# Converting twelve more weight pieces during attention, and moving the second output step, in a fused attention and bilinear FFN kernel on one Trainium2 core

## The chip, the core and the metric

The kernel runs on one core of a Trainium2 chip. The metric is the device time of one execution in microseconds (us). A core has five engines that each take their instructions in a fixed order: PE (TensorE, matrix products), DVE (VectorE), ACT (ScalarE), POOL (GpSimd) and SP (SyncE, which here issues most DMAs). They meet through semaphores: an instruction that waits holds up everything behind it on its engine.

## The reference

```python
scores = scale * q @ k.T                      # 8 batches, 8 heads, 576 tokens, head size 64
mask   = pos[:, None] // 64 >= pos[None] // 64
attn   = softmax(where(mask, scores, -1e9)) @ v
x      = attn.transpose(0, 2, 1, 3).reshape(4608, 512)
out    = ((x @ w_a) * (x @ w_b)) @ w_out      # w_a, w_b: 512 x 1536, w_out: 1536 x 512
```

q, k and v are float32. The three weights arrive as float64, and the kernel turns them into float32 itself, out of the bits. A float32 product is made of three products on PE, of a rounded part (`hi`) and the rest (`lo`) of each operand: hi·hi, hi·lo, lo·hi.

## The kernel before, in words

**Stages.** The 1536 columns of w_a and w_b (and the rows of w_out) are cut into twelve blocks of 128. First comes attention, 64 heads one behind the other; the first pass of the FFN (blocks 0 to 3) is woven into it, so that PE always has products to do between the steps of a head. When attention is over, a rest of the first pass is left (here the tail). Then comes pass 0 (blocks 4 to 7) and pass 1 (blocks 8 to 11), each over six tiles of 768 tokens. A pass reads x and the partial output of the pass before from DRAM and writes its own. In a tile `pair_unit` (L696 to L738) makes 42 products of 384 columns per block, with DVE combining the results in between (the `u_z` operations, L726 to L736), and `pair_out` makes the output product, 96 matmuls (L754), whose results DVE adds to the partial output (L813).

**A head** has four kinds of work. `softmax`: scores on PE (L392, L412), maxima on DVE (L398), exponentials on ACT (L401), the sums' reciprocal `rc` on DVE (L442), then five scalings by `rc` on POOL (L445). `turn`: transposes of the scaled rows on PE (`tp`, L468), a rounded copy `ah` on ACT (L470), the rest `al` on DVE (L472). `values`: the output product in two steps, the first with `ah` (L517), the second with `al` (L521, L523). And the next pairs' K and Q are loaded by SP, split by ACT, DVE and POOL (L337 to L345, K's tile has one buffer) and copied by SP to where PE wants them (L358, L359). The table `SLOT` says in which order a slot of one head calls the steps of its own softmax, of the head before and of the one before that. The framework's scheduler then fixes each engine's order from it.

**Conversion.** A piece is 128 x 512 weights: per block two pieces of w_a and w_b (`KP` = 2) and one of w_out. `fetch` loads it, `convert` takes five DVE instructions (L139, L143, L145, L147, L149) and one of ACT (L140). For w_out, and for blocks 0 to 3, `split` makes hi (ACT) and lo. For w_a and w_b of later blocks `sums` makes four sums of columns (L172) and two instructions for lo (L177, L178). `convert_w` is a generator; each place that calls it lets it go on by a step, which is one DVE instruction or a few. `behind_of` puts a conversion's instruction behind a marked one in DVE's order, without a wait.

**Who converts what, before.** Blocks 0 to 3 in the first slots of attention. w_a and w_b of blocks 4 to 7 (8 pieces) from the end of attention through the tail, then w_out of 4 to 7 (4 pieces) within tile 0 of pass 0. In tiles 1 to 4 of pass 0 the twelve pieces of blocks 8 to 11, which go through a staging tile `st` to DRAM (`wabd`, `wod`) and come back at the end of pass 0. The lines that set the pace:

```python
STEP, STEP2 = 800, 1600                     # ns of PE time per step of conversion
background(min(k * HT / 2.4 / STEP, F2 * PER_F))
conv = convert_w(parts(range(F1 + F2, NF)), nc.vector, paced=True, stage=stage)
SLOT = [(S_, 0, 3), (S_, -1, 0), (T_, -2, 4), (S_, 0, 4), (V_, -2, 3), (S_, 0, 3),
        (T_, -1, 4), (V_, -2, 3), (S_, 0, 3), (T_, -1, 5), (T_, -1, 4)]
```

Of the kernel before, what the change touches and what calls it, by code (L numbers as in the profile page):

```python
# [41 lines left out]
STEP2 = 1600  # L42
# [10 lines left out]
def attention_then_bilinear_ffn(  # L53
# [33 lines left out]
    wod = dram.tile([F2, P, 2 * DO], F32, name="wod")  # L87
# [39 lines left out]
    def convert(raw, nm, paced):  # L127

        hi, mid = raw[:, :, 1], raw.bitcast(U16)[:, :, 1]
        s, m, x = (wpool.tile([P, 512], I32, tag=f"cv_{x}", name=f"{x}{nm}") for x in "smx")  # L130
        sf, mf, xf = (t.bitcast(F32) for t in (s, m, x))
        v = nc.vector

        def step(ins):
            if paced:
                behind_of(ins, "hf")
# [12 lines left out]
        step(v.tensor_tensor(xf, mf, sf, op=ALU.mult))  # L149
        return xf, mf  # L150
# [4 lines left out]
    def parts(fs):  # L155
        return [(f, i) for f in fs for i in range(KP)] + [(f, KP) for f in fs]
# [4 lines left out]
    def sums(hi, lo, xf, t, paced):  # L161
# [11 lines left out]
        if paced:  # L173
            behind_of(ins, "hf")
        nc.scalar.copy(hi[:, 3:], t)
        yield
        v.tensor_tensor(lo[:, :3], x[:, 1:], f32(hi[:, :3]), op=ALU.subtract)  # L177
        v.tensor_tensor(lo[:, 3:], t, f32(hi[:, 3:]), op=ALU.subtract)  # L178

    def convert_w(todo, lo_eng, paced=False, stage=None):  # L180
# [5 lines left out]
        for k, (f, i) in enumerate(todo):  # L186
            now, raw = raw, ahead(*todo[k + 1]) if k + 1 < len(todo) else None
            xf, spare = yield from convert(now, f"w{f}_{i}", paced)
            if stage:
                st = stage.tile([P, 2, NW if i < KP else NO, P], F32R, tag="st", name=f"st{f}_{i}")  # L190
            if i == KP:
                if not stage and w_sb[f][1] is None:
                    new_wo(f)
                o = st.rearrange("p j c n -> p j (c n)") if stage else w_sb[f][1]
# [383 lines left out]
    n_moe = n_conv = 0  # L578
# [4 lines left out]
    def want(now):  # L583

        n = (now - H - LAG) * per_slot - behind
        if now < 2 * H + LAG:
# [9 lines left out]
            (T_, -1, 4), (V_, -2, 3), (S_, 0, 3), (T_, -1, 5), (T_, -1, 4)]  # L596
    fill = sum(m for _, _, m in SLOT)
    gens = {}
    for s in range(NH + LAG):
# [11 lines left out]
        for g, m in steps:  # L611
# [43 lines left out]
    upool = pool(right, "upool", 2, "right", reuse_waits="tile")  # L655

# [113 lines left out]
    conv = convert_w(parts(range(F1, F1 + F2)), nc.vector, paced=True)  # L770
# [16 lines left out]
    stage = pool(left, "stage", 1, reuse_waits="tile")  # L787
# [12 lines left out]
    for ps_ in range(2):  # L800
        fs = list(range(F1 + ps_ * F2, F1 + (ps_ + 1) * F2))
        for tt in range(NT2):
# [19 lines left out]
            for i, f in enumerate(fs):  # L822
# [13 lines left out]
                if ps_ == 0 and tt == NT2 - 1:  # L836
                    new_w(f + F2)
# [7 lines left out]
            if ps_ == 0 and tt == 0:  # L845
                background(1e4)
                conv = convert_w(parts(range(F1 + F2, NF)), nc.vector, paced=True, stage=stage)
                n_conv, start, k, pace = 0, 0, 0, STEP2
            pair_out(fs, hs, nm, out)
            if ps_ == 0 and tt == NT2 - 1:  # L850
                background(1e4)
                for f in fs:
                    new_wo(f + F2)
                    nc.sync.dma_start(f32(w_sb[f + F2][1]).rearrange("p j n -> p (j n)"), wod[f - F1])
# [39 lines left out]
```

## Time and profile before

| | us |
|---|---|
| median of three runs | 1281.07 (1278.56 to 1282.27) |
| the profiled execution, its own time | 1281.83 |
| its span, first to last instruction | 1279.8 |
| PE busy | 1239.3 (97%) |
| DVE busy | 999.2 (78%) |
| ACT busy | 683.6 (53%) |
| POOL busy | 554.9 (43%) |

The times are of one profiled execution. A busy engine has an instruction in work; PE's instructions overlap, so a busy PE may still be slower than it could be, and the number of matmuls in a stretch tells more. Idle time of an engine that nobody waits for costs nothing. Attention takes about half of the span, the tail some 70 us, pass 0 the stretch from 699 us to 1000 us, and pass 1 the rest.

### The profile page before, as it was taken

How to read it: one execution, taken by the hardware profiler on the slowest of the kernel's cores; microseconds unless marked ns; L12 is line 12 of the kernel's file. 1: busy time of each engine (PE TensorE's matmuls, PEld its weight loads, DVE VectorE, ACT ScalarE, POOL GpSimd, SP SyncE). 2: the span in 40 equal slices, each digit the busy share in tenths (PEclk: the TensorE clock that was granted, in tenths of full speed). 3: DMA queues.
4: the chain of work that ended last, by engine and by line, in shares of the span. 5: the costliest groups of instructions: out<-in, count | busy, mean ns of one | idle time of the engine just before them, and what ended most of it. 6: DMA issues, size and time to landing. Idle time of an engine off the chain costs nothing.

```text
span 1279.8 us, 23524 instructions
## 1 busy us (share of the span) xinstructions
PE 1239.3 (97%) x7849; PEld 1173.2 (92%) x7849; DVE 999.2 (78%) x2389; ACT 683.6 (53%) x1722; POOL 554.9 (43%) x679
## 2 busy tenths in 40 slices
PE   9988999999999999999988998999999999999998
PEld 5668998999999999999988998999999999999998
DVE  6878887777887877877699999899967577577553
ACT  5788787788787788888745423233222222122210
POOL 4567565566665565665422322223223123123231
PEclk8999999999999999999998999999999999999999
DMA  5467766777767767676225355364466442243131
GB/s 195 132 167 201 187 174 175 178 171 181 170 167 179 179 171 176 167 178 155 87 94 171 100 180 194 139 206 164 141 220 244 145 149 79 70 149 98 52 99 62
DMA packets 93496, 196.58 MB, mean 154 GB/s; under 512 B 11968, under 2 KB 52928, under 8 KB 93376
## 3 DMA queue, kind: packets, MB, share of 16 engines
q1 hardware_dynamic: 88768, 185.64, 51.4%
q10 hardware_dynamic: 4608, 9.44, 2.0%
q8 instruction: 63, 1.03, 0.3%
q14 instruction: 57, 0.47, 0.1%
HBM read 96.47 MB, written 47.19 MB: 112 GB/s over the span
## 4 chain that ended last, share of the span: by engine, by line
PE 71%; DVE 15%; DMA 4%; issue 4%; ACT 3%; POOL 2%; SPq 1%; ACTq 0%; DVEq 0%; POOLq 0%
PE pso_z L754 13%; PE ps L217 12%; PE tp L468 7%; PE psx_z L708 6%; PE psw_z L708 6%; PE psv_z L708 6%; PE pso L217 4%; PE s L392 4%; PE psy_z L708 3%; PE av L517 3%; PE av L523 3%; PE sl L392 2%; DMA kp<-kT 2%; PE av L507 2%; DVE sw L147 1%
## 5 line engine op out<-in xcount | busy, mean ns | idle before, releaser
L113 POOL TENSOR_TENSOR h_z<-u_z,h_z 128x384 fp32r<-128x384 f32 x96 | 112.8, 1175 | 391.4 <-ACT h_z L110 379.8
L217 PE MATMUL ps<-xh,wab 128*128 128x288 f32 x1024 | 241.8, 304 | 1.2 <-ACT a L241 1.2
L754 PE MATMUL pso_z<-h_z,wo 128*128 128x384 f32 x1152 | 204.0, 335 | 4.5 <-POOL h_z L113 4.5
L445 POOL TENSOR_SCALAR e<-e,rc 128x512 f32<-128x512 f32 (+3 forms) x256 | 151.6, 604 | 127.9 <-DVE rc L442 118.1
L754 PEld LDWEIGHTS pso_z<-h_z,wo 128*128 128x128 f32 x1152 | 199.6, 188 | 7.0 <-POOL h_z L113 7.0
L217 PEld LDWEIGHTS ps<-xh,wab 128*128 128x128 f32 x1024 | 172.3, 189 | 4.7 <-ACT a L241 1.4
L472 DVE TENSOR_TENSOR al<-tp,ah 128x512 fp32r<-128x512 f32 x224 | 131.6, 608 | 31.5 <-ACT ah L470 31.0
L217 PE MATMUL ps<-xl,wab 128*128 128x288 f32 x512 | 154.1, 301 | 0.0
L468 PE MATMUL tp<-ident,e 128*128 128x128 f32 x832 | 136.1, 278 | 10.4 <-POOL e L445 4.0
L470 ACT CAST ah<-tp 128x512 fp32r<-128x512 f32 x224 | 116.4, 531 | 50.3 <-PE tp L468 47.5
L110 ACT CAST h_z<-u_z 128x384 fp32r<-128x384 f32 x96 | 49.3, 514 | 167.7 <-DVE u_z L733 160.2
L217 PE MATMUL pso<-hh,wo 128*128 128x288 f32 x512 | 128.1, 311 | 4.3 <-ACT hh L110 4.3
L708 PE MATMUL psx_z<-xh,wab 128*128 128x384 f32 x384 | 118.5, 344 | 7.2 <-DVE u_z L726 6.7
L468 PEld LDWEIGHTS tp<-ident,e 128*128 128x128 f32 x832 | 100.8, 142 | 25.7 <-POOL e L445 9.5
L401 ACT ACTIVATE e<-s,nm 128x192 f32<-128x192 f32 (+2 forms) x192 | 101.5, 529 | 32.4 <-DVE nm L398 23.2
L708 PE MATMUL psw_z<-xh,wab 128*128 128x384 f32 x384 | 117.0, 340 | 0.8 <-DVE u_z L728 0.8
L708 PE MATMUL psv_z<-xh,wab 128*128 128x384 f32 x384 | 116.7, 339 | 0.5 <-DVE u_z L730 0.4
L398 DVE TENSOR_REDUCE nm<-s 128x1 f32<-128x192 f32 (+3 forms) x256 | 109.9, 431 | 2.4
L217 PEld LDWEIGHTS ps<-xl,wab 128*128 128x128 f32 x512 | 96.5, 188 | 3.4
L217 PEld LDWEIGHTS pso<-hh,wo 128*128 128x128 f32 x512 | 88.3, 192 | 6.6 <-ACT hh L110 5.3
L113 POOL TENSOR_TENSOR v<-vr,v 128x320 fp32r<-128x320 f32 x56 | 50.2, 897 | 89.3 <-ACT v L110 67.9
L392 PE MATMUL s<-k,q 128*128 128x256 f32 x336 | 81.2, 322 | 2.2 <-ACT e_s L401 1.9
(142 smaller groups left out, 2919.5 us busy)
## 6 DMA issues: line engine op xcount, KB each, us to landing
k<-kp SPq DMA_DIRECT2D x112, 288.0 KB, 3.8
xr<-xd SPq DMA_DIRECT2D x48, 384.0 KB, 3.5
pt<-part SPq DMA_DIRECT2D x96, 192.0 KB, 3.5
q<-qp SPq DMA_DIRECT2D x112, 160.0 KB, 2.6
raww<-wab SPq DMA_DIRECT2D x24, 512.0 KB, 3.8
qp<-qT SPq DMA_DIRECT2D x32, 320.0 KB, 3.2
vr<-vm SPq DMA_DIRECT2D x64, 160.0 KB, 3.1
kp<-kT SPq DMA_DIRECT2D x32, 288.0 KB, 3.5
```

Source lines behind the costliest of these rows:

```text
L110: nc.scalar.copy(hi, src)
L113: return lo_eng.tensor_tensor(lo, src, f32(hi), op=ALU.subtract)
L217: mm = nc.tensor.matmul(ps, w_, d_, start=(i == 0), stop=(i == n - 1))
L392: mark = nc.tensor.matmul(ps[:, :w], qm[:, q0[t]:q0[t] + P], kk[:, :w], start=(i == 0), stop=(i == len(ks) - 1))
L398: nc.vector.tensor_reduce(nm[:, t:t + 1], view, axis=AX.X, op=ALU.max, negate=True)
L401: nc.scalar.activation(out, view, AF.Exp, bias=bias, accum_out=sm[:, t, :1])
L445: nc.gpsimd.tensor_scalar(ev, ev, rc[:, t:t + 1], 1.0, op0=ALU.mult, op1=ALU.mult)
L468: mark = nc.tensor.transpose(tp[:, c], src, ident)
L470: nc.scalar.copy(ah[:, :m, cols], tp[:, :m])
L472: return nc.vector.tensor_tensor(al[:, :m, cols], tp[:, :m], f32(ah[:, :m, cols]), op=ALU.subtract)
L708: nc.tensor.matmul(ps, wt[:, i, iw], j[:, ix], start=start and kp == 0 and i == 0 and j is xh, stop=kp == KP - 1 and i == 1, skip_group_ch ...
L754: nc.tensor.matmul(ps, wt[:, a, osl], b, start=i == 0, stop=i == 3 * len(fs) - 1)
```

## The change

Twelve of the twenty-four later pieces are converted during attention and kept in DRAM: w_out of blocks 4 to 11 (8 pieces) and w_a, w_b of blocks 8 and 9 (4 pieces). A new generator `convert_to_dram` does it, from slot 13 to the last, by steps spread evenly, behind the marked `rc`. It has no tile of its own: hi is written to the second buffer of the raw tile, lo in place over the converted values, and both are stored by SP in two or three DMAs. w_out of blocks 4 to 7 is then loaded by `load_wo`. In pass 0 only w_a, w_b of blocks 10 and 11 (4 pieces) are left, at 3000 instead of 1600 ns per step. In `SLOT` the second step of `values` of the head before last now stands in front of a step of `turn` of the last head, instead of behind it.

```diff
-STEP2 = 1600
+STEP2 = 3000
...
-    wod = dram.tile([F2, P, 2 * DO], F32, name="wod")
+    wod = dram.tile([2 * F2, P, 2 * DO], F32, name="wod")
...
+    def convert_to_dram(todo, paced):
+
+        for f, i in todo:
+            raw = fetch(wab[f, :, i] if i < KP else wo[f], f"w{f}_{i}")
+            yield
+            xf, spare = yield from convert(raw, f"w{f}_{i}", paced)
+            n = f"st{f}_{i}"
+            hi = wpool.tile([P, 2 * NO, P], F32R, tag="raw", name=n, bufs=2)
+            if i == KP:
+                hi = hi[:, :NO].rearrange("p c n -> p (c n)")
+                lo = xf.bitcast(F32R)
+                split(hi, lo, xf, nc.scalar, nc.vector)
+                nc.sync.dma_start(wod[f - F1, :, :DO], f32(hi))
+                nc.sync.dma_start(wod[f - F1, :, DO:], f32(lo))
+            else:
+                hi = hi[:, :NW]
+                lo = yield from sums(hi, None, xf, spare, paced)
+                to = wabd[f - F1 - F2, i]
+                nc.sync.dma_start(to[:, :NW * P], f32(hi).rearrange("p c n -> p (c n)"))
+                nc.sync.dma_start(to[:, NW * P:][:, :3 * P], f32(lo[0]).rearrange("p c n -> p (c n)"))
+                nc.sync.dma_start(to[:, (NW + 3) * P:], f32(lo[1]).rearrange("p c n -> p (c n)"))
+            yield
...
+    HALF = F1 + F2 + F2 // 2
+    later = convert_to_dram(parts(range(F1, NF), [KP]) + parts(range(F1 + F2, HALF), range(KP)), "rc")
+    LATER_FROM, LATER_STEPS = 13, 2 * F2 * 6 + F2 // 2 * KP * 7
...
-            (T_, -1, 4), (V_, -2, 3), (S_, 0, 3), (T_, -1, 5), (T_, -1, 4)]
+            (V_, -2, 3), (T_, -1, 4), (S_, 0, 3), (T_, -1, 5), (T_, -1, 4)]
...
+            while k in (6, 9) and n_later < LATER_STEPS * (now - LATER_FROM) / (NH - 1 - LATER_FROM):
+                next(later, None)
+                n_later += 1
...
+    def load_wo(f):
+        new_wo(f)
+        nc.sync.dma_start(f32(w_sb[f][1]).rearrange("p j n -> p (j n)"), wod[f - F1])
...
-    conv = convert_w(parts(range(F1, F1 + F2)), nc.vector, paced=True)
+    conv = convert_w(parts(range(F1, F1 + F2), range(KP)), nc.vector, paced="hf")
...
+    for f in range(F1, F1 + F2):
+        load_wo(f)
...
-                conv = convert_w(parts(range(F1 + F2, NF)), nc.vector, paced=True, stage=stage)
+                conv = convert_to_dram(parts(range(HALF, NF), range(KP)), "hf")
```

What this does to the engines' orders is shown at three places. Names carry buffer numbers, which differ between the two programs, and the change's lines are about 20 to 35 higher.

PE in the slot of a head in the middle of attention, before: `s` are scores, `ps` products of the first pass, `tp` transposes of the last head, `av` the output product of the head before it.

```order
L392 MATMUL s_0_4618<-k_0_4405,q_0_4404 128x320 x2
L217 MATMUL ps_2_1_1_4678<-xh_0_1_2656,wab_81 128x288
L217 MATMUL ps_2_1_1_4678<-xh_1_1_2974,wab_81 128x288
L217 MATMUL ps_2_1_1_4678<-xl_1_1_2975,wab_81 128x288
L468 MATMUL tp_7_3_4695<-ident,e_3_120 128x128 x4
L217 MATMUL ps_2_1_1_4678<-xh_1_1_2974,wab_81 128x288
L217 MATMUL ps_2_1_1_4678<-xh_2_1_3292,wab_81 128x288
L217 MATMUL ps_2_1_1_4678<-xl_2_1_3293,wab_81 128x288
L217 MATMUL ps_2_1_1_4678<-xh_2_1_3292,wab_81 128x288
L521 MATMUL av_6_4706<-ah_6_4534,v_6_4491 128x128
L521 MATMUL av_6_4706<-al_6_4535,v_6_4491 128x128
L523 MATMUL av_6_4670<-al_6_4535,v_6_4491 128x256
```

The same engine in the same slot with the change:

```order
L542 MATMUL av_6_4767<-ah_6_4634,v_6_4564 128x128
L542 MATMUL av_6_4767<-al_6_4635,v_6_4564 128x128
L544 MATMUL av_6_4744<-al_6_4635,v_6_4564 128x256
L544 MATMUL av_6_4744<-al_6_4635,v_6_4564 128x320
L544 MATMUL av_6_4744<-al_6_4635,v_6_4564 128x448
L544 MATMUL av_6_4744<-al_6_4635,v_6_4564 128x512
L238 MATMUL ps_2_1_1_4752<-xh_1_1_2994,wab_81 128x288
L238 MATMUL ps_2_1_1_4752<-xh_2_1_3321,wab_81 128x288
L238 MATMUL ps_2_1_1_4752<-xl_2_1_3322,wab_81 128x288
L489 MATMUL tp_7_3_4792<-ident,e_3_120 128x128 x4
```

The six matmuls of the second output step, which stood behind the first four transposes, now stand in front of them.

DVE in that slot with the change, from the last `al` of one head to the first maximum behind it (`xf` and `avlo` belong to `values`, `hf` to the first pass, `xw` and the line with `st` to a w_out piece):

```order
L493 TENSOR_TENSOR al_6_4635<-tp_6_0_4721,ah_6_4634 128x2x128
L451 MEMSET s_0_4692 64x64
L359 SCALAR_TENSOR_TENSOR qp_2_4360<-qp_2_4360 128x640
L419 TENSOR_REDUCE nm_0_4688<-s_0_4692 128x1
L549 TENSOR_TENSOR xf_3_4743<-av_6_4767,avlo_6_4774 64x64
L550 TENSOR_TENSOR avlo_6_4774<-av_6_4767,avlo_6_4774 64x64
L149 TENSOR_TENSOR xw_2_4307<-mw_2_4306,sw_2_4305 128x512
L552 TENSOR_TENSOR avlo_6_4774<-avlo_6_4774 64x64
L553 TENSOR_TENSOR xf_3_4743<-av_6_4744,avlo_6_4774 64x512
L493 TENSOR_TENSOR al_7_4791<-tp_7_3_4792,ah_7_4790 128x4x128
L113 TENSOR_TENSOR xw_2_4307<-xw_2_4307,st_2_4782 128x512
L451 MEMSET s_0_4808 64x64
```

Two conversion instructions (L149 and L113) are added in this slot; both stand behind the `al` that the second output step needs, and the rest of the work is as before. On ACT, the copy of K (L344) stands behind the first transpose copy of a head in twenty pairs before, and behind the third or the last with the change.

DVE in tile 0 of pass 0, second block, before (`u_z` combines products of `pair_unit`; `sw`, `mw`, `xw` and the line that writes `wo` are the conversion of w_out):

```order
L726 TENSOR_TENSOR u_z_0_5_10719<-psx_z_0_5_10676,u_z_0_5_10719 128x384
L113 TENSOR_TENSOR wo_10652<-xw_2_10614,wo_10652 128x512
L736 TENSOR_TENSOR u_z_0_4_10628<-psx_z_0_4_10561,u_z_0_4_10628 128x384
L139 TENSOR_SCALAR sw_2_10680<-raww_2_10610 128x512
L143 TENSOR_SCALAR mw_2_10681<-raww_2_10610 128x512
L728 TENSOR_TENSOR u_z_0_5_10720<-psw_z_0_5_10677,u_z_0_5_10719 128x384
L145 SCALAR_TENSOR_TENSOR mw_2_10681<-raww_2_10610,mw_2_10681 128x512
L147 SCALAR_TENSOR_TENSOR sw_2_10680<-raww_2_10610,sw_2_10680 128x512
L730 TENSOR_TENSOR u_z_0_5_10720<-psv_z_0_5_10678,u_z_0_5_10720 128x384
```

And with the change (`xt` and `xr` prepare the next tile's x):

```order
L760 TENSOR_TENSOR u_z_0_5_10888<-psx_z_0_5_10857,u_z_0_5_10888 128x384
L762 TENSOR_TENSOR u_z_0_5_10889<-psw_z_0_5_10858,u_z_0_5_10888 128x384
L764 TENSOR_TENSOR u_z_0_5_10889<-psv_z_0_5_10859,u_z_0_5_10889 128x384
L709 TENSOR_TENSOR xt_1_1_11079<-xr_1_10854,xr_1_10852 128x384
L710 TENSOR_TENSOR xr_1_10852<-xr_1_10852 128x384
```

The conversion has left the stretch between the combining steps. Over pass 0, DVE's order holds 30, 23, 29, 26, 16 and 0 conversion rows in tiles 0 to 5 before, and 2, 12, 16, 10, 0 and 0 with the change. The tail's order differs by four rows, the switch from pass 0 to pass 1 by none.

## Rows read from the trace of the kernel before

**Rows 1.** Busy time by stretch: attention; pass 0, tiles 0 to 4; a tile of pass 1.

```profile
core 0: us, PE busy (x) PEld busy (x) DVE busy (x) ACT busy (x) POOL busy (x), PEclk, DMA share, GB/s
218.00:618.00 400.00, 398.20 (x2871) 381.98 (x2870) 316.86 (x1006) 320.50 (x903) 245.03 (x350) 1.00 0.68 169
...
699.00:747.00 48.00, 47.11 (x264) 45.70 (x263) 47.62 (x83) 19.46 (x33) 14.65 (x11) 1.00 0.44 142
747.00:800.00 53.00, 47.64 (x266) 45.51 (x266) 48.97 (x86) 17.63 (x30) 13.58 (x10) 1.00 0.53 176
800.00:848.50 48.50, 47.26 (x265) 45.49 (x264) 43.66 (x76) 15.55 (x27) 13.52 (x10) 1.00 0.49 157
848.50:897.40 48.90, 47.32 (x267) 45.62 (x266) 46.53 (x81) 17.05 (x29) 13.49 (x10) 1.00 0.54 187
897.40:945.80 48.40, 47.48 (x266) 45.60 (x265) 41.62 (x63) 13.11 (x23) 13.47 (x10) 1.00 0.47 151
...
1043.90:1090.40 46.50, 46.50 (x267) 46.33 (x266) 31.37 (x51) 11.37 (x20) 13.14 (x10) 1.00 0.35 107
```

**Rows 2.** Groups by line and shape, whole span: busy us, mean ns of one.

```profile
L145 DVE SCALAR_TENSOR_TENSOR mw<-raww,mw 128x512 f32<-128x512 uint16 x36 | 32.5, 902 | 0.4
L147 DVE SCALAR_TENSOR_TENSOR sw<-raww,sw 128x512 int32<-128x512 int32 x36 | 29.9, 829 | 0.7 <-ACT sw L140 0.6
L149 DVE TENSOR_TENSOR xw<-mw,sw 128x512 f32<-128x512 f32 x36 | 28.2, 783 | 0.7
L140 ACT ACTIVATE sw<-sw,shift 128x512 int32<-128x512 int32 x36 | 26.0, 723 | 13.7 <-DVE sw L139 13.3
L143 DVE TENSOR_SCALAR mw<-raww 128x512 int32<-128x512 int32 x36 | 23.2, 644 | 0.1
L139 DVE TENSOR_SCALAR sw<-raww 128x512 int32<-128x512 int32 x36 | 20.0, 556 | 0.1
L172 DVE TENSOR_TENSOR mw<-xw 128x128 f32<-128x128 f32 x32 | 9.0, 320 | 0.2
L178 DVE TENSOR_TENSOR st<-mw,st 128x512 fp32r<-128x512 f32 x8 | 5.8, 726 | 0.2 <-ACT st L175 0.2
L177 DVE TENSOR_TENSOR st<-xw,st 128x384 fp32r<-128x384 f32 x8 | 4.4, 546 | 0.0
L113 DVE TENSOR_TENSOR st<-xw,st 128x512 fp32r<-128x512 f32 x4 | 2.8, 690 | 0.3 <-ACT st L110 0.3
```

**Rows 3.** Waits of DVE in attention, 218 to 618 us: us, times, longest.

```profile
DVE al L472 <- ACT ah L470: 20.7, 25, 1.2
DVE s L413 <- PE s L412: 15.6, 30, 1.1
DVE avlo L531 <- ACT avlo L530: 7.7, 18, 0.7
DVE xf L528 <- ACT avlo L527: 7.1, 19, 0.4
DVE nm L398 <- PE sl L392: 4.7, 30, 0.2
```

**Rows 4.** Timeline of one head's slot: start us, us, instruction, idle before.

```profile
524.08 0.19 DVE L442 RECIPROCAL rc<-rc 128x5 f32<-128x5 f32 x1
524.19 0.98 DVE L472 TENSOR_TENSOR al<-tp,ah 128x512 fp32r<-128x512 f32 x2
...
524.37 1.31 POOL L445 TENSOR_SCALAR e<-e,rc 128x512 f32<-128x512 f32 x2 [3.14 <-DVE rc L442]
...
525.71 0.60 PE L468 MATMUL tp<-ident,e 128*128 128x128 f32 x4
526.68 0.22 PE L521 MATMUL av<-ah,v 128*128 128x128 f32 x1
```

**Rows 5.** One POOL group at 60 to 112 us and at 218 to 618 us.

```profile
L445 POOL TENSOR_SCALAR e<-e,rc 128x448 f32<-128x448 f32 x5 | 4.5, 907 | 0.0
...
L445 POOL TENSOR_SCALAR e<-e,rc 128x448 f32<-128x448 f32 x41 | 26.3, 641 | 0.0
```

**Rows 6.** DMA issues, whole span: count, KB each, median us to landing.

```profile
raww<-wab SPq DMA_DIRECT2D x24, 512.0 KB, 3.8
```

More of the change, by code (lines that the diff above doesn't have):

```diff
@@ L135, in step @@
             if paced:
-                behind_of(ins, "hf")
+                behind_of(ins, paced)
         step(v.tensor_scalar(s, hi, 20, 0x7FF, op0=ALU.logical_shift_right, op1=ALU.bitwise_and))
@@ L153, in attention_then_bilinear_ffn, with parts @@
     w_sb = {}
-    def parts(fs):
-        return [(f, i) for f in fs for i in range(KP)] + [(f, KP) for f in fs]
+    def parts(fs, which=range(KP + 1)):
+        return [(f, i) for f in fs for i in which if i < KP] + [(f, i) for f in fs for i in which if i == KP]
     def new_wo(f):
@@ L173, in sums, with convert_w @@
         if paced:
-            behind_of(ins, "hf")
+            behind_of(ins, paced)
         nc.scalar.copy(hi[:, 3:], t)
         yield
-        v.tensor_tensor(lo[:, :3], x[:, 1:], f32(hi[:, :3]), op=ALU.subtract)
-        v.tensor_tensor(lo[:, 3:], t, f32(hi[:, 3:]), op=ALU.subtract)
-    def convert_w(todo, lo_eng, paced=False, stage=None):
+        if lo is None:
+            lo = x[:, 1:].bitcast(F32R), t.bitcast(F32R)
+        else:
+            lo = lo[:, :3], lo[:, 3:]
+        v.tensor_tensor(lo[0], x[:, 1:], f32(hi[:, :3]), op=ALU.subtract)
+        v.tensor_tensor(lo[1], t, f32(hi[:, 3:]), op=ALU.subtract)
+        return lo
+    def convert_w(todo, lo_eng, paced=None):
         def ahead(f, i):
@@ L188, in convert_w @@
             xf, spare = yield from convert(now, f"w{f}_{i}", paced)
-            if stage:
-                st = stage.tile([P, 2, NW if i < KP else NO, P], F32R, tag="st", name=f"st{f}_{i}")
             if i == KP:
-                if not stage and w_sb[f][1] is None:
-                    new_wo(f)
-                o = st.rearrange("p j c n -> p j (c n)") if stage else w_sb[f][1]
+                o = w_sb[f][1]
                 split(o[:, 0], o[:, 1], xf, nc.scalar, lo_eng)
@@ L577, in attention_then_bilinear_ffn @@
     conv = convert_w(parts(range(F1)), nc.gpsimd)
-    n_moe = n_conv = 0
+    HALF = F1 + F2 + F2 // 2
+    later = convert_to_dram(parts(range(F1, NF), [KP]) + parts(range(F1 + F2, HALF), range(KP)), "rc")
+    LATER_FROM, LATER_STEPS = 13, 2 * F2 * 6 + F2 // 2 * KP * 7
+    n_moe = n_conv = n_later = 0
     for p in range(2):
@@ L637, in attention_then_bilinear_ffn @@
                 n_moe += 1
+    for _ in later:
+        pass
     order.close()
@@ L786, in attention_then_bilinear_ffn @@
     ppool = pool(left, "ppool", 6, reuse_waits="tile")
-    stage = pool(left, "stage", 1, reuse_waits="tile")
     xs = []
@@ L836, in attention_then_bilinear_ffn @@
                 if ps_ == 0 and tt == NT2 - 1:
+                    background(1e4)
                     new_w(f + F2)
@@ L850, in attention_then_bilinear_ffn @@
             if ps_ == 0 and tt == NT2 - 1:
-                background(1e4)
                 for f in fs:
-                    new_wo(f + F2)
-                    nc.sync.dma_start(f32(w_sb[f + F2][1]).rearrange("p j n -> p (j n)"), wod[f - F1])
+                    load_wo(f + F2)
     left.close()
```

6 lines of the change are left out of this document (2 added, 4 removed).

## The prediction

> **What bounds the kernel now.** I read the busy times by stretch first. In attention PE is busy 398.2 of 400 us [rows 1], so 1.8 us in 400 is all that PE stands idle there, and DVE (316.9) and ACT (320.5) are below 81%. In pass 1 a tile of 264 matmuls or a few more takes 46.5 us, PE is never idle and DVE is busy 31.4 us of them [rows 1]. The same matmuls take 48.0, 53.0, 48.5, 48.9 and 48.4 us in tiles 0 to 4 of pass 0 [rows 1], where DVE is busy 41.6 to 49.0 us. So PE sets the pace in attention and in pass 1, and DVE slows it in pass 0. The reader is to see two things: the excess over 46.5 us goes with DVE's load (6.5 us in the tile with 49.0 us of DVE, none with 31.4), and the granted clock is 1.00 in all these stretches, so it explains nothing. Then I read the groups by line for the price of a conversion [rows 2], the waits of DVE in attention for the room that it has there [rows 3], and the timeline of one head for who waits for it [rows 4].
>
> **What pass 0 gets back.** The excess of tiles 0 to 4 is 1.5 + 6.5 + 2.0 + 2.4 + 1.9 = 14.3 us [rows 1]. DVE's work without conversion is the 31.4 us of a pass 1 tile, so conversion takes 16.3, 17.6, 12.3, 15.2 and 10.3 us in the five tiles. The orders keep 2 of 30, 12 of 23, 16 of 29, 10 of 26 and 0 of 16 conversion rows. In proportion DVE is then busy 32.5, 40.6, 38.2, 37.2 and 31.4 us. What is left of the excess I take on a straight line between the two least loaded tiles, 31.4 us with none and 41.6 us with 1.9 [rows 1], or 0.19 us per us of DVE: 0.2 + 1.7 + 1.3 + 1.1 + 0 = 4.3. The gain is 14.3 - 4.3 = **10.0 us**. Upper end: all of the excess, 14.3. Lower end: tile 1, whose excess is out of line with the others, keeps its 6.5 us for another reason (the combining of x for the next tile, say), which leaves 10.0 - 4.8 = 5.2. Tile 5 has no conversion before or after, and at the switch of passes the orders are the same, so I take nothing there. In the tail the eight pieces of blocks 4 to 7 stay, so nothing there either.
>
> w_out of blocks 4 to 7 is now loaded, four loads of 512 KB. One such load lands 3.8 us after its issue [rows 6], so even one behind the other they need 15 us. They are first used when 168 of the tile's 264 matmuls are done, 168/264 of 46.5 = 29.6 us after its start: I cost them at nothing. Without that cover PE would wait up to 15 us.
>
> **What attention pays on DVE.** The five instructions of a conversion take 0.902 + 0.829 + 0.783 + 0.644 + 0.556 = 3.71 us [rows 2]. With lo (0.69) a piece of w_out costs 4.40 us. With four sums (0.32 each), 0.55 and 0.73 for lo, a piece of w_a and w_b costs 6.27 us [rows 2]. Eight and four of them are 35.2 + 25.1 = 60.3 us, over the 50 slots from 13 on **1.21 us per head**. A head takes 400/41 = 9.76 us (41 heads by the count of their scalings in that stretch [rows 5]), DVE is busy 7.73 us of it and idle 2.03. Not all idle time can be filled; what the waits of [rows 3] hold is 55.8 us, 1.36 per head, of which PE ends 0.50 and ACT 0.87. The order shows that the added instructions stand behind the `al` that PE waits for, so they delay only the next maxima, and these begin with a wait for PE. 1.36 is more than 1.21, so on average the conversion fits. It does not where a step is long: the multiplication and four sums of a w_a piece go out together, 0.78 + 4 x 0.32 = 2.06 us, 0.70 more than the waits of a head. Four such steps: **2.8 us**. Lower end 0; upper end: only the waits that PE ends can be filled, 0.72 us short per head, 36 us.
>
> **ACT, SP and the swap.** On ACT the twelve pieces add 28 instructions of at most 0.72 us (its first [rows 2] is the longest), 0.40 us per head; ACT is idle (400 - 320.5)/41 = 1.94 us per head [rows 1], which hides it. SP gets 12 loads and 28 stores in attention, and the loads of K stand behind some of them: two of the twelve raw loads stand directly in front of one. Upper end: 3.8 us each [rows 6], 7.6 us; lower end 0. I take **1.5 us**, near the lower end, because ACT's copy of K stands later in the head than before (in most pairs behind the third or last copy of the transposes, where it stood behind the first). The swap can return no more than PE's idle time, 1.8 us in 400 [rows 1]; I count nothing. What it moves is room. The first scaling of POOL starts 0.1 us behind `rc` and, as half of 1.31 us, ends at 525.02; the transposes start at 525.71, so they had 0.69 us to spare [rows 4]. They now come one output step later. The output step had 526.68 - 525.17 = 1.51 us behind its `al` and moves up by at most 526.68 - 525.71 = 0.97, so 0.54 is left.
>
> **The port between DVE and POOL.** While conversion ran in the first slots, POOL's 448-wide scaling took 907 ns, against 641 without it [rows 5]; this is 0.27 us on a chain with 0.69 us to spare and more behind the swap, so by the rows it costs nothing. The Trainium skill (SBUF — State Buffer, section "SBUF: two separate sides") has a stronger rule, and it speaks against the change: a DVE instruction with two SBUF inputs and a POOL instruction exclude each other for the whole of an instruction, and the loser blocks fully. By that rule the time would be rival B's, below, 10.5 us above mine.
>
> **The sum.** 1281.83 (the profiled execution; 1279.8 of span and 2.0 around it) - 10.0 + 2.8 + 1.5 = 1276.1 us. The median of the runs is 0.8 below that execution, so I say **1275 us**.
>
> **Rivals.** A, slower: DVE becomes the bound of attention. The waits that ACT ends do not get filled, because ACT's copies themselves come later when DVE and then PE are later. If half of them fill, DVE lacks 1.21 - 0.50 - 0.43 = 0.28 us per head, 14 us in 50 heads; if none, 36. It decides against the change when the room that fills is below 1.04 us per head (10.0 - 1.5 = 8.5 us of gain over 50 heads is 0.17). Against it: 1.36 us of waits per head, and PE idle for 1.8 us only. For it: pass 0 shows PE losing 2 us per tile at a DVE load of 90%, and attention would go from 79% to 92%. Time: 1281.83 - 10.0 + 1.5 + 14 - 0.8 = 1286.5, and up to 1308.
>
> B, also slower: POOL's first scaling is held up by a whole conversion instruction, up to 0.90 us [rows 2] in each of 50 heads, and the swap's room does not help, since PE now stops one group earlier, at the second output step. 0.90 - 0.69 = 0.21 us, 10.5 us in all: 1276.1 + 10.5 - 0.8 = 1285.8. For it: the 907 ns. Against it: conversion does not stand right behind `rc` in DVE's order.
>
> C, no change: tile 1 keeps its excess, so that pass 0 gives 5.2 us, and attention takes 4.3 back: 1281.83 - 5.2 + 4.3 - 0.8 = 1280.1. For it: what PE waits for in tile 1 may be a backlog from the tail, which stays.
>
> **Chances.** My forecast 0.53, A 0.20, B 0.07, C 0.20. About 0.3%, 3.8 us, is what a measurement here can tell from no change. The forecast counts as faster: 0.53. C and a little of A's low end count as the same: 0.22. The rest of A, and B, as slower: 0.25. The low end of the range is all of the excess gained and nothing paid: 1281.83 - 14.3 - 0.8 = 1266.7, so 1267. The high end takes in B and the lower part of A: 1291. Faster and no change hold most of the chance; the forecast alone would reach from 1267 to 1278.
>
> **What the profile after would show.** Right, if tiles 0 to 4 take about 46.7, 48.2, 47.8, 47.6 and 46.5 us, with DVE at 31 to 41 us, and if a head in the middle of attention keeps 9.8 us, with DVE busy about 8.9 of them and its waits nearly gone. A shows as heads of 10 us or more, with PE idle before transposes or the second output step, released by DVE. B shows as scalings of 0.9 us and PE waits that POOL ends. C shows as tile 1 still above 52 us. I am wrong altogether if PE waits for w_out in tile 0 (a DMA as releaser at about 726 us), or if K's copies come late and ACT stands idle for a DMA.

## The result

The changed kernel took 1290.44 us (median of 6 runs, 1285.51 to 1292.26), the kernel before 1279.80 in its six runs beside it. The ratio is 1.0077 with a 95% interval of 1.0052 to 1.0103: slower by 9.9 us by the ratio, where 1275 us and faster was forecast.

Where the time went is read from the two traces at four marks: the last head's `rc`, the start of pass 0, the start of pass 1, the end.

| us | before | after | difference |
|---|---|---|---|
| start to the last head's `rc` | 628.6 | 649.7 | +21.1 |
| from there to pass 0 (tail) | 70.2 | 70.9 | +0.7 |
| pass 0 | 294.8 | 281.5 | -13.3 |
| pass 1 | 286.2 | 288.4 | +2.2 |
| span | 1279.8 | 1290.5 | +10.7 |

Pass 0 gave more than forecast, attention cost 21 us instead of 4. First the busy times by stretch of the kernel after: attention, tiles 0 to 4 of pass 0, a tile of pass 1.

```profile
core 0: us, PE busy (x) PEld busy (x) DVE busy (x) ACT busy (x) POOL busy (x), PEclk, DMA share, GB/s
218.00:628.80 410.80, 393.18 (x2805) 372.44 (x2804) 348.42 (x1057) 326.63 (x902) 265.49 (x340) 1.00 0.72 192
720.58:767.04 46.46, 46.46 (x266) 46.29 (x265) 35.88 (x58) 15.15 (x26) 15.26 (x12) 1.00 0.43 141
767.04:814.18 47.14, 47.00 (x265) 46.06 (x265) 38.86 (x63) 13.18 (x23) 13.24 (x10) 1.00 0.41 129
814.18:861.11 46.93, 46.82 (x266) 46.20 (x266) 38.72 (x66) 13.98 (x26) 13.77 (x10) 1.00 0.42 130
861.11:907.87 46.76, 46.44 (x265) 45.66 (x265) 40.67 (x67) 13.48 (x24) 13.86 (x10) 1.00 0.48 158
907.87:954.34 46.47, 46.47 (x266) 46.30 (x265) 27.68 (x43) 9.19 (x17) 13.17 (x10) 1.00 0.33 98
...
1056.00:1102.50 46.50, 46.50 (x266) 46.34 (x265) 31.33 (x50) 11.37 (x20) 13.16 (x10) 1.00 0.34 103
```

Against [rows 1], tile 1 fell from 53.0 to 47.1 us, and what is left of the excess over 46.5 is 0.6 + 0.4 + 0.3 = 1.3 us. In attention PE is now idle for 17.6 of 410.8 us, where it was 1.8 of 400. DVE is busy for 85%, so no engine is full. PE's waits there (us in total, times, longest):

```profile
PE tp L489 <- DVE s L451: 7.7, 11, 1.3
PE tp L489 <- DVE s L434: 4.2, 9, 0.6
PE tp L489 <- DVE al L493: 3.4, 7, 1.3
PE tp L489 <- POOL e L466: 0.7, 2, 0.5
PE tp L489 <- POOL v L113: 0.6, 1, 0.6
```

All of them are transposes (`tp`). They do not use what L451 or L434 write (the masks of the scores); these small instructions are only the next ones on DVE behind the `al` that frees a transposes' buffer. There are two such buffers, and in the order of the change a head's third group of transposes needs the first group's `al`; why in this order, and not in the one before, is shown with the swap alone below. One such wait in the timeline of the kernel after (start us, us, instruction, idle before):

```profile
376.64 0.91 PE L544 MATMUL av<-al,v 128*128 128x256 f32 x4
...
377.60 0.72 ACT L140 ACTIVATE sw<-sw,shift 128x512 int32<-128x512 int32 x1
...
377.78 0.60 PE L489 MATMUL tp<-ident,e 128*128 128x128 f32 x4
...
378.34 0.53 ACT L422 ACTIVATE e<-s,nm 128x320 f32<-128x320 f32 x1
...
378.99 0.58 ACT L551 COPY avlo<-av 64x512 f32<-64x512 f32 x1
...
379.60 0.59 ACT L491 CAST ah<-tp 128x512 fp32r<-128x512 f32 x1
379.60 0.22 DVE L552 TENSOR_TENSOR avlo<-avlo 64x64 f32<-64x64 f32 x1 [1.35 <-ACT avlo L551]
...
379.92 0.69 DVE L553 TENSOR_TENSOR xf<-av,avlo 64x512 f32<-64x512 f32 x1
...
380.64 0.69 DVE L493 TENSOR_TENSOR al<-tp,ah 128x512 fp32r<-128x512 f32 x1
...
381.48 0.52 PE L489 MATMUL tp<-ident,e 128*128 128x128 f32 x3 [0.80 <-DVE s L451]
```

The first transposes end at 378.38. Their copy `ah` starts 1.2 us later, because ACT first does the conversion's shift (L140), an exponential and the output's `avlo`. On DVE the `al` stands behind the combining of the output (L552, L553), which waits for that `avlo`. The `al` ends at 381.33, the transposes start 0.15 us behind it, and PE has stood still for 0.80 us. (Where the profile names the `al` itself, as in the second fence on the swap alone below, the transposes start as far behind it: 0.14 us.) Three things are in that chain: the swap (it puts the output's step in front), a conversion instruction on ACT, and others on DVE in other heads. The experiments take them apart.

### The profile page after: what moved, and what is told of

It is laid out like the page before. It is cut to its first block, busy times and chain, and to the rows that moved or that the text cites. A ratio compares the mean times of both kernels' runs of the same rounds, so it can differ in the third digit from the quotient of the medians.

```text
span 1290.5 us, 23526 instructions
## 1 busy us (share of the span) xinstructions
PE 1239.9 (96%) x7849; PEld 1175.8 (91%) x7849; DVE 994.5 (77%) x2389; ACT 682.0 (53%) x1722; POOL 589.8 (46%) x679
## 4 chain that ended last, share of the span: by engine, by line
PE 62%; DVE 20%; ACT 6%; issue 5%; DMA 4%; POOL 3%; SPq 0%; DVEq 0%; ACTq 0%; POOLq 0%
PE pso_z L788 15%; PE psx_z L742 8%; PE psw_z L742 7%; PE psv_z L742 7%; PE ps L238 6%; PE tp L489 4%; DVE nm L419 4%; DVE al L493 4%; PE psy_z L742 4%; PE pso L238 3%; PE s L413 2%; ACT e L422 2%; DVE xf L553 2%; DMA q<-qp 1%; PE sl L413 1%
## 5 line engine op out<-in xcount | busy, mean ns | idle before, releaser
L113 POOL TENSOR_TENSOR h_z<-u_z,h_z 128x384 fp32r<-128x384 f32 x96 | 112.5, 1172 | 387.1 <-ACT h_z L110 369.2
L466 POOL TENSOR_SCALAR e<-e,rc 128x512 f32<-128x512 f32 (+3 forms) x256 | 177.4, 706 | 102.8 <-DVE rc L463 96.0
L489 PEld LDWEIGHTS tp<-ident,e 128*128 128x128 f32 x832 | 96.9, 141 | 52.8 <-issue 32.5
L419 DVE TENSOR_REDUCE nm<-s 128x1 f32<-128x128 f32 (+3 forms) x256 | 109.4, 429 | 2.5
L113 POOL TENSOR_TENSOR hl<-hf,hh 128x288 fp32r<-128x288 f32 x64 | 55.1, 861 | 80.2 <-ACT hh L110 80.2
```

What stands on the lines that cost most here:

```text
L113: return lo_eng.tensor_tensor(lo, src, f32(hi), op=ALU.subtract)
L419: nc.vector.tensor_reduce(nm[:, t:t + 1], view, axis=AX.X, op=ALU.max, negate=True)
L466: nc.gpsimd.tensor_scalar(ev, ev, rc[:, t:t + 1], 1.0, op0=ALU.mult, op1=ALU.mult)
L489: mark = nc.tensor.transpose(tp[:, c], src, ident)
```

## The experiments

A mark without the noise of the first heads is the time from the 31st to the last `rc`, 33 heads; it is named "33 heads" below (before: 319.6 us). Each edit lets the scheduler place other instructions anew too, so a difference belongs to the edit with the order that follows from it.

### The swap alone, and the conversion alone

```diff
 e1_no_swap (of the change), e2_swap_only (of before)
-            (V_, -2, 3), (T_, -1, 4), (S_, 0, 3), (T_, -1, 5), (T_, -1, 4)]
+            (T_, -1, 4), (V_, -2, 3), (S_, 0, 3), (T_, -1, 5), (T_, -1, 4)]
 e2 is the reverse of this
 e3_dma_only, in attention
-            xf, spare = yield from convert(raw, f"w{f}_{i}", paced)
...
+                for a, b in zip(cut, cut[1:]): nc.sync.dma_start(to[:, a:b], rf[:, :b - a])
...
```

> The change without the swap of the two slot entries, so that the second output step stands behind the first transposes as before; all conversion as in the change. Pass 0 of the changed kernel took 281.6 us against 294.8 before, so its gain is there whatever the order. Theory S (the swap): with the swap DVE's first al of a head stands behind the combining of the output (avlo, xf), which waits for ACT; a head fell from 9.76 to 10.2 us for that. Then heads of 9.8 us, no more PE waits before transposes than the 3 us of before, and 1270 to 1276 us. Theory L (the load of the conversion on DVE and ACT): the instructions themselves hold up the copies that PE waits for, whatever the order; heads of 10.1 to 10.3 us and 1287 to 1293 us. If the swap helps, as it was perhaps meant to, more than 1293.

> The kernel before with the swap of the two slot entries and nothing else. Theory S: heads of about 10.2 us, 18 to 22 us more in attention, 1295 to 1302 us. Theory L: the swap alone costs nothing, heads of 9.7 to 9.8 us, 1277 to 1283 us.

> The change with its loads and stores in attention, but without the conversion instructions on DVE and ACT there (the stores take resident weights, so the weights of blocks 4 to 11 that depend on these pieces, and the output, are not the reference's). The swap stays. Theory S: the swap alone keeps heads at 10.1 us or more, 1285 to 1292 us. Theory L: without the instructions heads are 9.8 us, 1268 to 1273 us. A third, that SP's 40 DMAs delay K: heads of 10 us with ACT waiting for a DMA.

Measured: without the swap 1297.45 us (1.0154, 1.0131 to 1.0178; 33 heads 341.0); the swap alone 1288.12 (1.0075, 1.0051 to 1.0099; 324.3); with the swap and the DMAs alone 1280.15 (1.001, 0.9992 to 1.0027; 324.3). The second and the third time lie in neither theory's range, and both theories were right in a part: the swap alone costs 9.6 us, and yet it saves 9.9 us (by the ratios) where the conversion is present. Between the two traces the swap alone makes the span 7.9 us longer, 5.5 us of it up to the last `rc`.

Which transposes need the first `al`? The second output step takes one of the two transposes' buffers too, for `av0`, its first two matmuls (L460 and L519 of the kernel before):

```python
            tp = ps_t.tile([P, 4, P], F32, tag="tp", name=f"tp{n}_{t}", bufs=2)
...
            av0 = ps_t.tile([P, 512], F32, tag="tp", name=f"av0{n}", bufs=2)
```

If the two are handed out in turn, the second transposes get the first ones' buffer before, because `av0` lies between them, and the third ones get it with the swap, because `av0` then comes first. The traces agree. In the last 54 heads of the kernel before, the second transposes never start less than 0.14 us behind the end of the first `al`, and within 0.2 us in 2 heads. With the swap alone they start before that end in all 54, and it is the third that never start less than 0.14 us behind it, and within 0.2 us in 27 heads (in the change in 40). One head before (behind [rows 4]) and one with the swap alone, in the same place:

```profile
527.02 0.69 DVE L472 TENSOR_TENSOR al<-tp,ah 128x512 fp32r<-128x512 f32 x1 [0.58 <-ACT ah L470]
...
528.80 0.60 PE L468 MATMUL tp<-ident,e 128*128 128x128 f32 x4
...
529.91 0.49 PE L468 MATMUL tp<-ident,e 128*128 128x128 f32 x3
```

```profile
450.69 0.60 PE L468 MATMUL tp<-ident,e 128*128 128x128 f32 x4
...
451.00 0.59 ACT L530 COPY avlo<-av 64x512 f32<-64x512 f32 x1
...
451.48 0.46 ACT L110 CAST v<-vr 128x320 fp32r<-128x320 f32 x1
...
451.84 0.74 ACT L337 ACTIVATE qp<-qp 128x640 fp32r<-128x640 f32 x1
...
452.47 0.60 PE L468 MATMUL tp<-ident,e 128*128 128x128 f32 x4
...
452.61 0.59 ACT L470 CAST ah<-tp 128x512 fp32r<-128x512 f32 x1
...
453.23 0.69 DVE L472 TENSOR_TENSOR al<-tp,ah 128x512 fp32r<-128x512 f32 x1 [0.48 <-ACT ah L470]
...
454.06 0.52 PE L468 MATMUL tp<-ident,e 128*128 128x128 f32 x3 [0.34 <-DVE al L472]
```

Before, the first `al` ends at 527.71 and the second transposes, which need it, start at 528.80, 1.09 us behind it. With the swap it ends at 453.92, when the second transposes have long started (452.47), and the third start 0.14 us behind it: PE has waited for it. From the first transposes to the ones that need their buffer there were 3.09 us and are now 3.37; but the `al` is ready 3.23 us behind the first transposes' start instead of 2.00, because ACT's `ah` comes behind `avlo`, and in this head behind the work on V and Q too.

### What of the conversion costs

```diff
 e4_behind_al
...
+                if t == LAST: last["al"] = ins
...
-    later = convert_to_dram(parts(range(F1, NF), [KP]) + parts(range(F1 + F2, HALF), range(KP)), "rc")
+    later = convert_to_dram(parts(range(F1, NF), [KP]) + parts(range(F1 + F2, HALF), range(KP)), "al")
...
-            while k in (6, 9) and n_later < ...
+            while k in (7, 10) and n_later < ...
...
 e5_no_act (e15_no_act_no_swap: the same without the swap)
+        if paced != "rc": nc.scalar.activation(s, s, AF.Relu, scale=2.0 ** 23, bias=shift)
...
+                nc.vector.tensor_tensor(hi, xf, xf, op=ALU.subtract) if paced == "rc" else split(hi, lo, xf, nc.scalar, nc.vector)
...
 e11_al_first: the output's combining behind the first al in DVE's order
+                if t == LAST and "out" in heads: tc.add_manual_dep(heads.pop("out").ins, ins.ins.name, NOSYNC, reason="al first")
...
+            heads["out"] = nc.vector.tensor_tensor(lo[:, W - BLK:], lo[:, W - BLK:], lo0[:, BLK:], op=ALU.add)
```

> The change with the 28 ACT instructions of the conversion in attention left out (the exponent's shift and the rounded copies; the weights made from these pieces, and the output, are not the reference's); DVE's instructions and the DMAs stay, in number and place. With the DMAs alone the kernel took 1280 us, the change 1290. If ACT's instructions delay the copies (ah, avlo) that DVE and PE wait for, 1280 to 1284 us, and DVE's waits for avlo fall. If it is DVE, 1286 to 1291 us.

> The loads and stores alone in attention, without the conversion instructions there and without the swap (the output is not the reference's). Pass 0 has its 13 us either way. If the swap costs by itself what it cost in the kernel before, 8 to 10 us, this falls from 1280 to 1268 to 1273 us, the time that the change could have had. If the DMAs delay Q and K by themselves, as they did in two heads at 223 and 245 us with the swap, 1276 us or more, with ACT waiting for Q's loads.

Measured: without ACT's instructions 1285.05 us (1.005, 1.0034 to 1.0066; 33 heads 331.9); the DMAs alone without the swap 1269.41 (0.9921, 0.9894 to 0.9948; 318.8). With the change's 33 heads at 335.1, the account is, by the ratios times 1280 us and by the 33 heads:

| added to the kernel before, one behind the other | us | 33 heads |
|---|---|---|
| lighter pass 0, 40 DMAs in attention (e8) | -10.1 | -0.8 |
| the swap (e3 less e8) | +11.4 | +5.5 |
| DVE's conversion instructions (e5 less e3) | +5.1 | +7.6 |
| ACT's conversion instructions (after less e5) | +3.5 | +3.2 |
| the change | +9.9 | +15.5 |

The 3.5 us of ACT's instructions are not clear of the two intervals. The DMAs of attention cost nothing without the swap: 33 heads of 318.8 against 319.6. With the swap they did cost something in the earlier heads: in e3's trace ACT stood 2.6 and 1.8 us before K's tile at 222 and 244 us, and PE 4.3 us behind it for `ah`. The change's trace has one such wait of ACT, 1.4 us, and none of PE behind it, so how the cost of attention splits between the swap and the conversion depends on the mark.

> The change (with the swap), but the conversion's instructions ordered behind the first al of a head, which frees the transposes' buffer that PE waits for, and emitted one step later; in the change one or two of them stand directly in front of that al in most heads. The same work in all. Theory P (place): PE waits because they stand in front of that al; heads fall from 10.15 us to the 9.85 of the swap alone, 1279 to 1284 us. Theory V (volume): DVE and ACT have no room for 1.2 us more per head wherever they stand, 1288 to 1293 us.

Measured: 1303.12 us (1.0174, 1.0147 to 1.0201; 33 heads 338.2). That is outside both ranges, and the place theory is not borne out: PE still waits for an `al`, 9.3 us in 310 to 620 us. The edit also calls the conversion one step later in the slot; why the time is 12.4 us above the change's is not settled.

> The change, swap and all, with one order on DVE turned round: the last two combining steps of the output (avlo, xf), which wait for ACT's copy, stand behind the first al of the next head instead of in front of it. In the trace of the change that al ends 5.8 us behind rc and PE's third transposes, which need its buffer, start 0.15 us later; without the swap it ends at 3.65 and they start at 5.71. Theory D (the swap costs because that al waits behind the combining): al ends 0.6 to 1.3 us earlier, PE's waits before transposes, 16 us in the second half of attention, fall by half or more, and the time falls by most of the swap's 10 us: 1279 to 1284 us. If what PE lacks is the two transposes' buffers and the products between them, whatever DVE's order, 1287 to 1292 us.

Measured: 1328.87 us (1.0386, 1.0362 to 1.0411; 33 heads 365.4), far outside both. In the last 33 heads that `al` ended 5.74 us behind its head's `rc` (median), in the change 5.37: no earlier. DVE now waits in front of it for ACT's `ah`, 25.4 us where the change has 8.6, so theory D is not borne out. But the new order has a fault of its own, and the test is not clean: on DVE a conversion stands waiting for the load of its raw weights, and everything behind it with it. DVE's waits in 310 to 620 us:

```profile
DVE al L493 <- ACT ah L491: 25.4, 19, 2.5
DVE sw L139 <- DMA raww<-wo: 10.6, 3, 4.3
DVE sw L139 <- DMA raww<-wab: 5.0, 1, 5.0
```

(The expectation names the third transposes for the heads without the swap too; there it is the second that need that buffer.)

### Why it costs 28 us without the swap

Without the swap ACT waited for Q's load in every other pair, 15.9 us in six pairs in 310 to 620 us; in the change it does not wait for Q there. One of them, in the run without the swap:

```profile
361.93 0.40 ACT L575 COPY ob<-pso 128x288 f32<-128x288 f32 x1
364.39 0.74 ACT L358 ACTIVATE qp<-qp 128x640 fp32r<-128x640 f32 x1 [2.06 <-DMA qp<-qT]
364.75 0.33 ACTq L560 DMA_DIRECT2D xd<-xf  x1
365.04 0.75 ACT L110 CAST xh<-xf 128x288 fp32r<-128x288 f32 x2
365.70 0.63 ACT L422 ACTIVATE e<-s,nm 128x448 f32<-128x448 f32 x1
...
366.46 0.50 PE L413 MATMUL s<-k,q 128*128 128x256 f32 x2 [0.74 <-ACT e L422]
```

The split of Q stands on ACT in front of the exponential of a score tile whose buffer PE needs next, and PE stood still for it (its products at 366.46 waited 0.74 us for that exponential). Q and K have one buffer each: load, split on ACT, DVE and POOL, spread by SP, next load is a loop of two heads, and in the kernel before Q landed only 0.0 to 1.1 us before ACT took it.

```diff
 e7_store_later (no swap): a step between split and store
+                split(hi, lo, xf, nc.scalar, nc.vector); yield
...
 e9_later_split, e10_eight_pieces (no swap)
-            if k == (3 if odd else 4) and s + 2 < NH:
+            if k == (3 if odd else 6) and s + 2 < NH:
...
 e14_no_qk_wait (no swap)
-        nc.scalar.mul(qp[:, 1].bitcast(F32R), qp[:, 0], SCALE)
+        nc.scalar.mul(qp[:, 1].bitcast(F32R), f32(w_sb[0][0]).rearrange("p j i c n -> p (j i c n)")[:, :SQ] if p >= 7 else qp[:, 0], SCALE)
...
```

> The change without the swap, each piece's stores issued one step later, when what they store is long done. Without the swap ACT waited 16 us for Q's loads in the second half of attention, in every other pair, and 1297 us was the time. If SP is held up by stores that wait for DVE and ACT (they waited up to 6.7 us), Q comes in time and the time falls to 1284 to 1290 us. If the loop of Q's one buffer (load, split, spread) is late because the splits on ACT, DVE and POOL are late, nothing changes: 1295 to 1299 us.

> All conversion of the change, no swap, and the splits of a pair's Q and K two steps later in their slot (after the seventh instead of the fifth step, the first spread after the ninth instead of the seventh), so that ACT reaches them some 2 us later; the spread copies had 11 us to spare. Without the swap and with the splits where they were, 1297 us, ACT waited 16 us for Q's loads in the second half of attention, and the fourth transposes came 2 to 3 us late in every other pair. Theory Q (ACT blocked by Q's load is most of the 28 us that conversion costs without the swap): 1278 to 1286 us, ACT's waits for that DMA gone. Theory V (volume on DVE and ACT): 1292 to 1298 us.

> The run without the swap (twelve pieces, 1297 us), where ACT's splits of Q and K from the seventh pair on read resident weights instead of the loaded Q and K (scores and output are not the reference's from there on); loads, spreads and all other work stay, and ACT no longer stands still until a load has landed. Theory Q (without the swap the cost of conversion is ACT standing before Q's late load, with the copies for PE behind it): 1276 to 1284 us. Theory V (the volume on DVE and ACT): 1292 to 1298 us, as before, with PE waiting for other copies.

> No swap, and the 28 ACT instructions of the conversion in attention left out (the output is not the reference's); DVE's instructions and the DMAs stay. With the DMAs alone the time was 1269 us, with everything 1297. With the swap DVE's part was 5 us and ACT's 5. If DVE's part is the same here, 1274 to 1278 us, and the rest comes from ACT's instructions; if DVE's instructions alone already make Q's loop late, 1288 us or more.

Measured: stores a step later 1307.1 us (1.0229, 1.0197 to 1.0262; 33 heads 349.6); later splits 1312.35 (1.0261, 1.0245 to 1.0278; 352.6); no wait for Q and K 1284.62 (1.0033, 1.0004 to 1.0063; 332.1); no ACT part 1293.46 (1.0116, 1.0082 to 1.0151; 339.5). The first two are misses: what lies later in the loop comes later too (in 310 to 620 us SP stood 63.9 and 61.5 us before POOL's K, where the run without the swap has 38.7), and with the later splits DVE waited for raw weights again, 9.4 us. The third stays just above its theory's 1284 (what ACT writes there is taken off again in the second part, so the parts still add up to Q and K): taking the wait away gives back 15.5 of the 29.8 us by the ratios (28 by the medians) that conversion costs there, about half. The fourth says that DVE's instructions alone make 25.0 of them, and ACT still waits for Q there, 12.6 us in 310 to 620 us. So they make the loop late, and the loop makes up half of the cost. Where the other half lies is not settled.

### Fewer pieces in attention

```diff
 e10, e13_eight_no_swap: w_out of blocks 8 to 11 goes to pass 0
-    later = convert_to_dram(parts(range(F1, NF), [KP]) + parts(range(F1 + F2, HALF), range(KP)), "rc")
+    later = convert_to_dram(parts(range(F1, F1 + F2), [KP]) + parts(range(F1 + F2, HALF), range(KP)), "rc")
...
-                conv = convert_to_dram(parts(range(HALF, NF), range(KP)), "hf")
+                conv = convert_to_dram(parts(range(HALF, NF), range(KP)) + parts(range(F1 + F2, NF), [KP]), "hf")
...
 e12_four_pieces: w_out of 4 to 7 in tile 0, as before
+    later = convert_to_dram(parts(range(F1 + F2, HALF), range(KP)), "rc")
...
+    conv = convert_w(parts(range(F1, F1 + F2)), nc.vector, paced="hf")
...
 e16_two_pieces: HALF = F1 + F2 + 1, STEP2 = 2200;  e17_none_in_attention: HALF = F1 + F2, STEP2 = 1700
```

> As the run with the later splits, but w_out of blocks 8 to 11 is converted in pass 0, whose tiles 1 to 4 have room (DVE busy 28 to 41 of 47 us in the change), so that eight pieces are left in attention (42.7 of 60.3 us of DVE, by the prices of the trace before). Pass 0 should pay 1 to 3 us. If the cost of conversion in attention goes with its volume or faster, attention pays 30 to 50 per cent less than in the run with the later splits: 1274 to 1281 us by theory Q, 1285 to 1291 us by theory V.

> Eight pieces in attention, as in the run that had the later splits too, but with the splits where they were before; no swap. With twelve pieces the later splits made it slower by 15 us; if they do so with eight, this gives 1278 to 1284 us instead of 1292; if they are neutral here, 1290 to 1294 us.

> No swap, and only four pieces in attention (w_a, w_b of blocks 8 and 9); w_out of 4 to 7 is converted in tile 0 of pass 0 as before, w_out of 8 to 11 and w_a, w_b of 10 and 11 in its later tiles. Pass 0 should gain 8 to 11 of its 13 us. With 12 pieces attention cost 26 us without the swap. If the cost is proportional to the pieces, 9 us: 1278 to 1281 us. If it rises faster than the pieces, as a queue that fills up would have it, 2 to 5 us: 1271 to 1276 us, faster than before.

> No swap, two pieces in attention (w_a, w_b of block 8) and ten in tiles 1 to 5 of pass 0 (2200 ns per step), w_out of 4 to 7 in tile 0 as before. With four pieces attention cost 7 us and pass 0 gave 11 us, 1275 us. If pass 0 only loses time where DVE is above some 41 us a tile, two more pieces (12.5 us of DVE over five tiles) cost 1 to 3 us there and attention gives back 3 to 4: 1272 to 1276 us. If pass 0 falls back to its old excess: 1278 us or more.

> No swap and no conversion in attention: all twelve later pieces in pass 0, as in the kernel before, but by the in-place generator without the staging tile and in its order (w_out last). This tells whether pass 0's 14 us of excess before came from the amount of conversion or from the staging tile and the order. Amount: tile 1 stays above 50 us and the time is 1277 to 1283 us. Staging and order: tiles 1 to 4 at 47 to 48 us, 1268 to 1273 us, and nothing had to move into attention.

| pieces in attention, no swap | us | ratio (95%) | 33 heads |
|---|---|---|---|
| 12 (e1) | 1297.45 | 1.0154 (1.0131 to 1.0178) | 341.0 |
| 8, later splits (e10) | 1292.21 | 1.0103 (1.0087 to 1.0119) | 339.1 |
| 8 (e13) | 1291.27 | 1.0093 (1.0066 to 1.0119) | 340.3 |
| 4 (e12) | 1275.16 | 0.9967 (0.9950 to 0.9984) | 323.5 |
| 2 (e16) | 1278.32 | 0.9981 (0.9964 to 0.9998) | 325.1 |
| 0 (e17) | 1270.71 | 0.9928 (0.9906 to 0.9949) | 318.9 |

The eight pieces missed: in the 33 heads they cost as much as twelve, in the whole time 7.8 us less, and the later splits are neutral there. Two and four can't be told apart; between four and eight the 33 heads jump by 17 us. The last run is the surprise: all twelve pieces are in pass 0 again, nothing is added to attention, and it is the fastest of the kernels that do all the work, 9.2 us below the one before. Its tiles 0 to 5:

```profile
695.00:742.80 47.80, 47.23 (x266) 45.89 (x265) 47.45 (x79) 20.09 (x34) 15.65 (x12) 1.00 0.41 132
742.80:790.10 47.30, 47.03 (x266) 45.77 (x265) 43.44 (x77) 14.59 (x27) 13.12 (x10) 1.00 0.48 153
790.10:837.80 47.70, 46.98 (x266) 46.04 (x265) 42.94 (x76) 16.05 (x29) 13.40 (x10) 1.00 0.48 158
837.80:886.20 48.40, 47.57 (x266) 45.90 (x265) 45.72 (x79) 15.64 (x27) 13.67 (x10) 1.00 0.58 197
886.20:933.50 47.30, 47.09 (x267) 46.14 (x266) 41.47 (x66) 13.52 (x24) 13.34 (x10) 1.00 0.49 151
933.50:981.90 48.40, 46.62 (x265) 45.77 (x264) 38.74 (x64) 14.95 (x25) 12.62 (x10) 1.00 0.85 296
```

Pass 0 takes 286.9 us; before it took 294.8, in the change 281.5. So 7.9 of the 13.3 us that pass 0 gained need no conversion in attention. They come from the other generator (in place, without the staging tile and without the next piece's load ahead) and the pace (1700 instead of 1600 ns per step, the last steps in tile 5); these were not separated. Moving the work into attention bought another 5.4 us there and cost 20 with the swap. Even the kernel that leaves the conversion in attention out and keeps its DMAs (e8, 1269.41 us) can't be told apart from this one.

## Why the prediction was wrong

**Pass 0: the size held, the reason only in part.** 10.0 us were forecast, 13.0 were gained in tiles 0 to 4. The step "the excess goes with DVE's load" is too simple: at 43.4, 42.9 and 41.5 us of DVE the last run loses 0.8, 1.2 and 0.8 us, where [rows 1] had 2.0 at 43.7 and 1.9 at 41.6. Tile 1's excess was no backlog from the tail: with tile 0 as before it fell to 47.1 us (four pieces), so rival C falls. The loads of w_out were hidden as said: tile 0 took 46.46 us.

**The swap: the step that failed most.** "I count nothing" stood on the first transposes' 0.69 us and the output step's 0.54 us to spare [rows 4]. These are the rooms of what the moved steps read; which buffers they write was left out. The moved output step holds one of the two transposes' buffers. So the swap passes the wait for the first `al` on from the second transposes, which had 1.09 us, to the third, and makes that `al` later, 1.23 us in the two heads shown; in half of the heads nothing is left. It costs 9.6 us alone, 11.4 beside the lighter pass 0.

**DVE in attention: 2.8 us forecast, 5.1 with the swap (7.6 in the 33 heads), 25.0 without.** "The added instructions stand behind the `al` that PE waits for" was misread: they stand behind the last `al` of one head, but the order's own rows have one (L149) in front of the next head's first `al`, the one that frees the buffer. And the room in DVE's waits [rows 3] is no room: a wait for ACT is filled only if ACT's work is not late as well.

**ACT: 0 forecast, 3.5 us with the swap and 4.9 without, neither clear of the intervals.** Its 28 instructions were called hidden in 1.94 us of idle time per head. Idle time is no slack where the next copy in order is waited for: in the timeline above the shift's 0.72 us stand in the chain that ends in PE's 0.80 us.

**SP: 1.5 us forecast, next to none seen in the change.** A load of K held ACT up once there, 1.4 us, and PE not; with the swap and the DMAs alone two did hold PE up. Q's came late without the swap, through the splits and not through the added DMAs, which alone cost nothing there.

**The rivals.** The time fell where A lay (1286.5 to 1308), with its sign: heads of 10.16 us from the 13th `rc` to the last, PE idle before transposes. But DVE did not become the bound (85% busy, 15.1 us of waits for `avlo` and 11.7 for `ah` left); the chain through two transposes' buffers did. By the whole times the swap is its larger half (11.4 of 20.0 us), by the 33 heads the conversion is (10.8 of 16.3). B's lengthening was there without B's effect. POOL's 448-wide scaling in attention, before in [rows 5], with the change:

```profile
L466 POOL TENSOR_SCALAR e<-e,rc 128x448 f32<-128x448 f32 x39 | 33.5, 858 | 0.0
```

That is 858 ns against 641, and 681 with the swap alone; PE's waits that a scaling ended are 0.7 us in all. The Trainium skill (SBUF — State Buffer, section "SBUF: two separate sides") has a DVE instruction with two SBUF inputs and a POOL instruction that reads SBUF exclude each other for a whole instruction. The trace agrees that POOL's work takes longer beside conversion; what a single instruction lost, no run here shows.

## What to carry to other kernels

Before a step is swapped, ask which buffers it and its neighbours take in turn, and read the room of the instruction that needs such a buffer in the new order, not only that of the step moved: here the moved step's own buffer decided who waits for whom. Idle time of an engine that works in order is room only if nothing queued behind the added instruction is waited for; two engines that wait for each other have less than either shows. And when a change does two things at once (here a cheaper way to convert, and another place for it), run the first without the second: it was the better kernel, 1270.71 us.

## What the runs showed of the hardware

The granted clock, as a mean over a stretch between its two levels of 1.2 and 2.4 GHz, was lowest in the run where PE stood still most. In 310 to 620 us it was 1.00 in the change, where PE was busy for 298 of 310 us, and 0.95 in the run with `al` first, where it was busy for 283. Between them it does not follow PE's busy time in order: it was 1.00 with 295 us (conversion behind the `al`) and 0.98 with 297 (eight pieces). The run with `al` first:

```profile
310.00:620.00 310.00, 283.32 (x1919) 266.43 (x1920) 244.58 (x728) 225.95 (x620) 178.08 (x232) 0.95 0.66 176
```

At the switch to pass 1 of the change DVE waited 3.4 us for x's load instead of 2.1, PE behind it 3.6 us instead of 2.1, and the clock was 0.93, against 0.97 before:

```profile
1002.10:1054.60 52.50, 48.92 (x267) 48.45 (x266) 34.69 (x57) 13.04 (x23) 13.17 (x10) 0.93 0.42 140
```

The longer wait is 1.5 of the 2.2 us that pass 1 lost. And the first two conversion instructions were cheaper in attention than their mean of the kernel before, 435 and 428 ns (L139, L143) against 556 and 644 [rows 2].
